# Seven products instead of eight in the second pass of a down projection

## The chip, the cores and the metric

The kernel runs on one core of a Trainium2 chip. The metric is the device time of one execution in microseconds (us). TensorE (PE; its weight loads are PEld) multiplies, VectorE (DVE), ScalarE (ACT) and GpSimd (POOL) work on elements, and SyncE (SP) issues nearly all DMAs from one queue. Every engine takes its instructions in the order of the program.

## The reference

```python
x = A_x                                   # (8192, 448), f32
xn = layernorm(x)
s = irfft2(shrink(relu(rfft2(xn) @ w1 + b1) @ w2 + b2))    # complex, 4 blocks of 112 channels
g = silu((gelu(xn @ w_gate) * (xn @ w_up)) @ w_down)       # 448 -> 1792 -> 448
return x + s * g
```

All arithmetic is as exact as f32: the kernel writes each f32 operand as the sum of two f16 numbers, "high" and "low", and a product as three f16 matmuls (high*high, high*low, low*high) that add up in PSUM.

## The kernel before

Two streams of work share TensorE.

The **feed-forward part** (`ffn`, `chunk`) goes over the tokens in 16 chunks of 512, twice. The first pass takes hidden features 0 to 1023 (8 blocks of 128), the second features 1024 to 1791 (6 blocks, three `unit`s of two blocks). A `unit` makes the up and gate projections of two blocks by a Winograd form of Strassen's scheme: seven products (`product`, a1 to a7) where the plain way has eight; the sums of operands are made beforehand. Its closing steps `c12` and `c21` apply GELU and the gating on ACT and DVE, and write the hidden tile `h` as high and low halves: a cast on ACT (`S.copy`), then a subtraction on DVE or POOL (`B.tensor_sub`). `down` then multiplies `h` with the down weights `dw0` and `dw1` (high, low). In the second pass a chunk has 4 token tiles x 6 blocks x 3 = 72 matmuls with 448 columns each, in `bd` banks. The first pass stores its sums to DRAM (`prt`); the second loads them (`pt_loads`, tile `pt`, two buffers), `ended` adds `bd` to them on DVE, takes tanh on ACT, multiplies on DVE and stores the result to DRAM (`gsp`). Each chunk's transposed tokens come by two transposing DMAs, `xta` and `xtb` (one buffer each).

The **spectral part** runs beside it in three phases. Phase 1 (first pass) normalizes and does the first Fourier stage. Phase 2 (`phase2`, most of the second pass) does the second stage and the spectral MLP in banks `bf`. Phase 3 (`phase3`) loads for each of 32 pairs of columns the spectrum `u2`, a table `mt`, the tokens `x2` and the gate `g2` (from `gsp`), multiplies, adds and stores to `out`. Each phase opens its own pools of tiles where those of the phase before stood.

The order on every engine is set by a planner (`Pace`) while the kernel is built: it keeps an estimated clock for each engine and for DMA (`cost`, line 128 and on), and emits an instruction when its estimate says that the inputs are there; `B` (`Either`) picks DVE or POOL, whichever it expects to end first. Phase 2 is spread evenly up to the planned time `END2`, phase 3 up to `END3`. All instructions are recorded through one helper, line 179, so groups are told apart by tile names.

Of the kernel before, what the change touches and what calls it, by code (L numbers as in the profile page):

```python
# [31 lines left out]
K1, K2 = 256, 192  # L32

# [196 lines left out]

def _split(a):
    hi = a.astype(np.float16)
    lo = (a - hi.astype(np.float64)).astype(np.float16)
    return hi, lo
# [91 lines left out]
def afno_geglu_kernel(ctx, tc, x, gu, wd, mlp, b1, b2, c_m, c_mt, c_small, out):  # L326
# [13 lines left out]
    dsp = nc.dram_tensor("dsp", (128, 2, PF[1][1], D), F16, kind="Internal").ap()  # L340
# [87 lines left out]
    YS = ring(p1, [128, 2, 2, D], F16, "ysb", 2)  # L428
# [5 lines left out]
    XTA = ring(fp, [128, XA // 128, 256], F16, "xta", 1)  # L434
# [7 lines left out]
    PT = ring(fp, [128, D], F32, "pt", 2)  # L442
# [84 lines left out]
    def stage1(c, q, xs):  # L527
# [6 lines left out]
        for a in range(2):  # L534
# [7 lines left out]
            S.activation(ysb[:, a, 0, :], py, AF.Copy, scale=2.0 ** -16)  # L542
            yield
            V.scalar_tensor_tensor(ysb[:, a, 1, :], py, 2.0 ** -16, ysb[:, a, 0, :],
                                   op0=ALU.mult, op1=ALU.subtract)
# [3 lines left out]
        for ri in range(2):  # L549
            Q.dma_start(t1[:, ri, n2:n2 + 2, :], ysb[64 * ri:64 * ri + 64].rearrange("p a s d -> p a (s d)"))  # L550
# [57 lines left out]
    def gu_block(b, to):  # L608
# [23 lines left out]
        S.activation(fc[:, 5, b:b + 1], half[:, 1:2], AF.Copy, scale=2.0 ** -25)  # L632
# [73 lines left out]
    def down_weights(p):  # L706
        fp0, nf = PF[p]
        if p == 0:

            parts, rings, kept = [(0, 4), (4, 2), (6, 2)], {0: WO, 4: XTB, 6: CB}, {}  # L710
        else:
            parts = [(fp0 + k, min(3, nf - k)) for k in range(0, nf, 3)]
# [25 lines left out]
        def split(f, n):  # L738
            t, v = yield from load(f, n)
            if p == 1:  # L740
                do = yield from WO.get()
                dv = do.rearrange("p s v c -> p (s v c)")[:, 0:2 * n * D].rearrange("p (s t c) -> p s t c", s=2, t=n)
            for i in range(n):
                d = [w[:, f + i] for w in dw] if p == 0 else [dv[:, s, i] for s in range(2)]
# [4 lines left out]
                if p == 0:  # L749
                    done("dw", f + i)  # L750
                yield
            (WS if p == 1 else rings[f]).put(t)
            if p == 1:
                Q.dma_start(dsp[:, :, f - fp0:f - fp0 + n, :], dv)
                WO.put(do)
# [18 lines left out]
        V.tensor_scalar(eguv[:, bs], eguv[:, bs], inv, 2.0 ** 14, op0=ALU.mult, op1=ALU.mult)  # L774
        V.tensor_scalar(cB[p], ED, 2.0 ** -11, None, op0=ALU.mult)
# [11 lines left out]
    def far_down():  # L787
        n = PF[1][1]
        for s in range(2):
            Q.dma_start(dw[s][:, 0:n], dsp[:, s])  # L790

    def prep_mlp():

        nonlocal f2, f20, ca, ca0, w1t, w2t, b1s, b2s
# [84 lines left out]
        rm.close()  # L879

# [40 lines left out]
    def glu(p, f0, gl, up, half, h, back):  # L921
        for cs, b in scaled(p, f0):
            V.scalar_tensor_tensor(gl[:, cs], up[:, cs], fc[:, 5, b:b + 1], gl[:, cs],
                                   op0=ALU.mult, op1=ALU.mult)
        back()
        yield
        v = gl.rearrange("p (e c) -> p e c", e=2)
# [5 lines left out]
    def unit(p, i, f0, h, xa, xb):  # L933
# [28 lines left out]
        def a2():  # L962
            m["Z"] = yield from BY.get()
            product(2, m["Z"], xb, f0, True, True)
# [10 lines left out]
        def a3():  # L975
            yield m["ep5"]
            product(3, m["Y"], xb, f0, False, True)
            pace.spawn(c12(), pace.last)

        def c12():  # L980
# [5 lines left out]
            yield m["c11"]  # L986
            yield from glu(p, f0, m["p1"], v, 0, h, lambda: V1.put(v))
# [19 lines left out]
        def a4():  # L1007
            yield m["ev2"]
            product(4, m["X"], xb, f0, False, True)
            pace.spawn(c21(), pace.last)  # L1010

        def c21():
            gl = yield from GL.get()
# [4 lines left out]
            yield from glu(p, f0, gl, m["v2"], 1, h, lambda: V2.put(m["v2"]))  # L1018
            GL.put(gl)
            done("h", p, i, f0, 1)  # L1020

        return [a1, a5, a6, a2, a3, a7], a4
# [40 lines left out]

    def pt_loads(i):
        for a in range(CH):
            t = yield from PT.get()
            Q.dma_start(t, prt[i][:, a * D:(a + 1) * D])
            yield
            EV["ptb", i, a] = t
            done("pt", i, a)  # L1070
# [21 lines left out]
    def ended(p, i, a, b, R):  # L1092
        ps = part(b, 128, D)
        if p == 0:
            th = yield from TH.get()
            S.activation(th, ps, AF.Copy, scale=cB[0])
            R.put(b)
# [640 lines left out]
```

## Time and profile before

| | us |
|---|---|
| median of three runs | 1840.76 (1838.62 to 1842.14) |
| profiled execution, its own time | 1841.37 |
| its span, first to last instruction | 1839.2 |
| TensorE busy | 1792.5 |
| VectorE busy | 1308.5 |
| ScalarE busy | 1061.2 |
| GpSimd busy | 351.6 |

The span is cut by the kernel's own stages: the first pass up to about 750 us; the second pass with phase 2 beside it up to 1500 us; the second pass with phase 3 beside it up to 1800 us; and an end in which the last chunk stands alone. A busy time of TensorE says how long it had a matmul under way; how long one matmul holds the engine is read from the distance between the starts of two groups that follow each other.

### The profile page before, as it was taken

What the parts mean: (1) busy time and instruction counts of PE and PEld (TensorE: products, weight loads), DVE (VectorE), ACT (ScalarE), POOL (GpSimd) and SP (SyncE); (2) the same over time, 40 slices, a digit from 0 to 9 for tenths busy, and PEclk for the clock granted to TensorE, in tenths of its full rate; (3) what the DMA queues carried; (4) which work ended last, traced back from release to release, by engine and by line L of the source; (5) the groups of instructions that cost most, each with busy time, mean ns of one, the idle gap of its engine ahead of it and who ended that gap; (6) DMA issues with size and microseconds to landing.
All of it is one profiled execution on the core that took longest, in us unless ns stands there. A gap on an engine that the chain in (4) does not pass through costs nothing. (4 is left out here: it accounts for less than half of the span.)

```text
span 1839.2 us, 36834 instructions
## 1 busy us (share of the span) xinstructions
PE 1792.5 (97%) x14785; PEld 1345.0 (73%) x14785; DVE 1308.5 (71%) x2271; ACT 1061.2 (58%) x2003; POOL 351.6 (19%) x425
## 2 busy tenths in 40 slices
PE   6999999999999999999999999999999999999998
PEld 3446667766777777787877887788877777777676
DVE  7867888778776665565767777787777766666656
ACT  4745656655555555576777766667766643333343
POOL 3434345325233123000100011010010100000000
PEclk9999999999999999999999999999999999999999
DMA  7463764766445533313235334343254349999872
GB/s 260 144 167 121 214 203 160 230 198 170 132 122 164 152 92 97 78 45 97 64 114 167 113 105 127 97 116 86 74 137 110 88 142 330 301 299 290 294 222 90
DMA packets 319196, 285.58 MB, mean 155 GB/s; under 512 B 230096, under 2 KB 286544, under 8 KB 319024
## 3 DMA queue, kind: packets, MB, share of 16 engines
q1 hardware_dynamic: 318880, 283.19, 52.3%
q8 instruction: 116, 1.90, 0.4%
q14 instruction: 56, 0.46, 0.1%
q10 hardware_dynamic: 144, 0.03, 0.0%
HBM read 128.44 MB, written 105.58 MB: 127 GB/s over the span
## 5 line engine op out<-in xcount | busy, mean ns | idle before, releaser
L179 PEld LDWEIGHTS <-wt 128*128 128x128 f16 x8582 | 836.0, 98 | 185.3 <-issue 19.8
L179 PE MATMUL bd<-dw,h 128*128 128x448 f16 x2592 | 528.6, 352 | 3.5 <-ACT th L179 2.5
L179 PE MATMUL bx<-xta,wt 128*128 128x256 f16 (+1 forms) x3843 | 475.7, 275 | 10.2 <-ACT u L179 4.3
L179 PEld LDWEIGHTS <-h 128*128 128x128 f16 x2592 | 249.9, 98 | 214.3 <-issue 4.1
L179 PE MATMUL by<-xtb,wt 128*128 128x256 f16 x2080 | 250.3, 273 | 0.0
L179 PE MATMUL by<-xta,wt 128*128 128x256 f16 (+1 forms) x1347 | 177.5, 281 | 7.1 <-DVE wt L179 3.1
L179 ACT COPY v<-bx 128x512 f32<-128x512 f32 x208 | 121.3, 583 | 90.9 <-PE bx L179 90.0
L179 DVE SCALAR_TENSOR_TENSOR gl<-v,fc,gl 128x512 f32<-128x512 f32 (+1 forms) x118 | 85.4, 733 | 88.0 <-ACT gl L179 87.3
L179 DVE TENSOR_TENSOR u<-by,u 128x512 f32<-128x512 f32 x104 | 71.6, 688 | 90.9 <-PE by L179 90.8
L179 PE MATMUL bx<-xtb,wt 128*128 128x256 f16 x1040 | 130.6, 273 | 0.3 <-ACT v L179 0.3
L179 POOL TENSOR_TENSOR zs<-t,zs 112x256 f16<-112x256 f32 (+1 forms) x40 | 33.9, 847 | 453.4 <-ACT zs L179 450.8
L179 ACT ACTIVATE gl<-bx,fc 128x512 f32<-128x512 f32 (+1 forms) x118 | 73.6, 637 | 76.4 <-PE bx L179 76.2
L179 ACT ACTIVATE u<-u,fc 128x512 f32<-128x512 f32 (+1 forms) x118 | 77.4, 667 | 60.2 <-DVE u L179 59.7
L179 ACT COPY u<-bx 128x512 f32<-128x512 f32 x104 | 60.7, 584 | 56.1 <-PE bx L179 55.9
L179 DVE SCALAR_TENSOR_TENSOR u<-v,fc,u 128x512 f32<-128x512 f32 (+1 forms) x118 | 87.4, 750 | 6.3 <-ACT u L179 0.8
L179 ACT COPY u<-by 128x512 f32<-128x512 f32 x104 | 60.9, 585 | 51.0 <-PE by L179 44.0
L179 ACT CAST h<-u 128x512 f16<-128x512 f32 x112 | 69.4, 620 | 26.6 <-DVE u L179 25.9
L179 PE MATMUL bf<-w2t,wn 112*128 112x112 f16 x1512 | 84.8, 213 | 0.0
L179 PEld LDWEIGHTS <-wn 112*128 112x128 f16 x1512 | 80.4, 98 | 5.5
L179 ACT ACTIVATE th<-pt 128x448 f32<-128x448 f32 x64 | 36.8, 576 | 77.0 <-DVE pt L179 76.7
L179 DVE SCALAR_TENSOR_TENSOR pt<-bd,fb,pt 128x448 f32<-128x448 f32 x64 | 43.6, 681 | 52.6 <-DMA pt<-prt 33.4
L179 ACT CAST h<-gl 128x512 f16<-128x512 f32 x104 | 64.4, 619 | 27.7 <-DVE gl L179 27.5
(188 smaller groups left out, 2607.0 us busy)
## 6 DMA issues: line engine op xcount, KB each, us to landing
wst<-in_gu SPq DMA_DIRECT2D x22, 704.0 KB, 5.6
xts<-sx SPq DMA_DIRECT2D x32, 480.0 KB, 2.9
x<-in_x SPq DMA_DIRECT2D x17, 896.0 KB, 6.3
t<-ysb SPq DMA_DIRECT2D x64, 224.0 KB, 3.4
prt<-th SPq DMA_DIRECT2D x64, 224.0 KB, 2.7
pt<-prt SPq DMA_DIRECT2D x64, 224.0 KB, 3.6
u<-t SPq DMA_DIRECT2D x32, 448.0 KB, 5.0
y<-t SPq DMA_DIRECT2D x15, 896.0 KB, 5.1
```

Of the source, the lines that this page charges most:

```text
L179: return self.pace.issue(self.name, kind, out, ins, lambda: fn(out, *args, **kw))
```

## The change

- The second pass's down projection takes Strassen's seven products. The hidden tile of two blocks and the two halves of 256 tokens are the left 2x2 matrix; the down weights of two blocks and the two halves of 224 output channels (`DH`) the right one. `factors2` makes the four sums of weights once and stores all seven to DRAM; `far_down` and `far_rest` load them into `dw0`, `dw1` and unused columns of `wt0` to `wt4`. A product of three pairs of blocks is 3 x 2 token tiles x 3 = 18 matmuls with 224 columns: 126 in a chunk.
- The four sums of hidden tiles are made in each unit by `sums`, in f32, in spare columns of `wt7`, and split into high and low halves in `wt6` and `h`. A product's bank is not summed in PSUM alone: `add2` adds a bank to the quarter of `pt` that it belongs to, seven times in a chunk where `ended` did it four times, and some banks go on accumulating after that.
- `down2` issues the first part of a chunk's products after its last unit; the rest (`tail`) stands inside the next chunk's first unit.
- `pt` and `gsp` go by quarters (two token tiles x 224 channels): `pt` has four buffers of half the size. `xta` has a second buffer from the end of phase 1 on, and its next load is issued at a chunk's start rather than at its end.
- Phase 3 has no `o2` buffers any more: its result is written over `g2`, and the store goes out of `g2`.
- Phase 2's planned end goes from 1440 to 1480, phase 3's from 1790 to 1780, and before pools are opened the planner waits 4 or 6 us after the last work. Phase 2's input `y` is loaded in halves of the channels.

```diff
+    def factors2(j, v, sc):
+        S.activation(v, v, AF.Copy, scale=sc)
...
+        B.tensor_sub(c[:, 0], b12, b11)
+        B.tensor_sub(c[:, 2], b22, b12)
+        yield
+        B.tensor_sub(c[:, 1], b22, c[:, 0])
+        yield
+        B.tensor_sub(c[:, 3], b21, c[:, 1])
...
+        Q.dma_start(dsp[:, :, 7 * DH * j:7 * DH * (j + 1)], dv)
...
+    def far_rest():
+        n = dw[0].shape[1] * 2
+        for k in range(n, 7 * PF[1][1] // 2):
+            for s in range(2):
+                Q.dma_start(right(k, s), dsp[:, s, DH * k:DH * k + DH])
...
+        PT = ring(mq, [128, 2, DH], F32, "pt", 4)
+        XTA.put(mq.tile([128, XA // 128, 256], F16, name="xta"))
...
+        def sums(gl):
+            yield ev("h", p, i, f0, 0)
+            g0, x = m["g0"], gl[:, 512:768]
+            a11, a12, a21, a22 = g0[:, 0:256], g0[:, 256:], gl[:, 0:256], gl[:, 256:512]
+            B.tensor_add(x, a21, a22)
+            S.copy(h[:, f0 + 1, 0, 256:], a22)
+            yield
+            B.tensor_sub(a21, a11, a21)
+            B.tensor_sub(a11, x, a11)
+            yield
+            B.tensor_sub(a12, a12, a11)
...
+            S.copy(w[0], v)
+            yield
+            S.copy(hs[0][:, 0], g0)
+            B.tensor_sub(w[1], v, w[0])
+            B.tensor_sub(h[:, f0 + 1, 1, 256:], a22, h[:, f0 + 1, 0, 256:])
...
+            B.tensor_sub(hs[1][:, 0], g0, hs[0][:, 0])
...
+    def prod2(k, i, h, bank_, j0, j1, first=False, last=False):
+        (e, c), r = PROD2[k]
+        for j in range(j0, j1):
...
+            for t in range(2):
+                for n, (s, v) in enumerate(((0, 0), (0, 1), (1, 0))):
+                    T.matmul(bank_[:, DH * t:DH * t + DH], w[s][:, 128 * t:128 * t + 128], right(7 * j + r, v),
+                             start=first and j == 0 and t == 0 and n == 0,
+                             stop=last and j == 2 and t == 1 and n == 2, skip_group_check=True)
+            yield pe()
+    def add2(i, q, bank_):
+        yield ev("pt", i, q)
+        t = EV["ptb", i, q]
+        V.scalar_tensor_tensor(t, part(bank_, 128, 2, DH), cB[1], t, op0=ALU.mult, op1=ALU.add)
+        yield
+    def down2(i, h, last):
+        yield from last()
+        x = yield from BD.get()
+        yield from prod2(1, i, h, x, 0, 2, first=True)
+        z = yield from BY.get()
+        yield from prod2(2, i, h, z, 0, 2, first=True)
+        y = yield from BD.get()
+        yield from prod2(5, i, h, y, 0, 2, first=True)
+        yield from prod2(1, i, h, x, 2, 3)
+        e = pace.spawn(add2(i, QS[0], x), pace.last)
+        yield from prod2(2, i, h, z, 2, 3, last=True)
+        yield e
+        pace.spawn(ended2(i, QS[0], z, BY), pace.last)
+        yield from prod2(6, i, h, x, 0, 2)
+        def tail():
+            yield from prod2(5, i, h, y, 2, 3)
+            e5 = pace.spawn(add2(i, QS[1], y), pace.last)
+            yield from prod2(6, i, h, x, 2, 3)
+            e = pace.spawn(add2(i, QS[2], x), pace.last)
+            yield e5
+            yield from prod2(3, i, h, y, 0, 2)
+            yield e
+            yield from prod2(7, i, h, x, 0, 3)
+            pace.spawn(ended2(i, QS[1], x, None), pace.last)
+            yield from prod2(3, i, h, y, 2, 3, last=True)
+            pace.spawn(ended2(i, QS[2], y, BD), pace.last)
+            yield ev("u3", i)
+            yield from prod2(4, i, h, x, 0, 3, last=True)
+            pace.spawn(ended2(i, QS[3], x, BD), pace.last)
...
         yield ev("xt", "a", p, i)
+        if p == 1 and nxt:
+            pace.spawn(xt_load(nxt[1], "a", nxt[0]))
...
             for n, s in enumerate(six):
+                if (u, n) == (0, 2) and "tail" in state:
+                    yield from state.pop("tail")()
...
-    END1, END2, END3 = T1 + NG * DT + 12.0, 1440.0, 1790.0
+    END1, END2, END3 = T1 + NG * DT + 12.0, 1480.0, 1780.0
...
-            V.scalar_tensor_tensor(o2[:, a, :], p, cF, t[3][:, a, :], op0=ALU.mult, op1=ALU.mult)
+            V.scalar_tensor_tensor(o2[:, a, :], p, cF, o2[:, a, :], op0=ALU.mult, op1=ALU.mult)
...
-            P3["g2"].put(t[3])
             Q.dma_start(ov[:, 2 * c:2 * c + 2, :], o2)
-            P3["o2"].put(o2)
+            P3["g2"].put(o2)
```

TensorE at the end of a chunk of the second pass, before. `bd` is the bank of the down projection, `h` the hidden tile (weights of the array), `dw0` and `dw1` the down weights; `vt` and `sm` belong to phase 2, `bx` and `xta` to the next chunk's first unit.

```order
L179 MATMUL bd_16424<-dw0_84,h_15680 128x448
L179 LDWEIGHTS h_15680
L179 MATMUL bd_16424<-dw1_85,h_15680 128x448
...
L179 LDWEIGHTS sm_4502
L179 MATMUL bf_16469<-vt_16413,sm_4502 128x448
...
L179 LDWEIGHTS wt0_76
L179 MATMUL bx_16481<-xta_16195,wt0_76 128x256
```

The chunk's down projection ends before the next chunk's first product. TensorE at such a place now, where product 2 ends in bank `by_13710` and product 6 goes on in bank `bd_13682`, which holds product 1; `wt6` holds sums of hidden tiles:

```order
L180 MATMUL by_13710<-dw0_84,h_12297 128x224
L180 LDWEIGHTS h_12297
L180 MATMUL by_13710<-dw1_85,h_12297 128x224
L180 LDWEIGHTS h_12297
L180 MATMUL by_13710<-dw0_84,h_12297 128x224
L180 LDWEIGHTS wt6_82
L180 MATMUL bd_13682<-dw0_84,wt6_82 128x224
```

Each matmul has half the columns and still its own weight load, and a bank goes on from `h` to the sums in `wt6`, after `add2` has read it.

SP in phase 3, before: one pair of columns' loads (`u2`, `mt`, `x2`, `g2`) and its store, with the second pass's `gsp`, `pt` and `xta` between.

```order
L179 DMA g2_20188<-gsp 128x896
L179 DMA out_0<-o2_20190 128x896
L179 DMA gsp<-th_20275 128x448
L179 DMA pt_20309<-prt 128x448
L179 DMA u2_20311<-t2 128x2x896
L179 DMA mt_20313<-c_mt 128x768
L179 DMA x2_20315<-in_x 128x896
L179 DMA g2_20317<-gsp 128x896
L179 DMA out_0<-o2_20319 128x896
L179 DMA_TRANSPOSE xta_20425<-xts 128x16x256
```

The same queue now; `g2` is both loaded and stored.

```order
L180 DMA pt_21120<-prt 128x2x224
L180 DMA_TRANSPOSE xtb_21148<-xts 128x9x256
L180 DMA g2_21163<-gsp 128x896
L180 DMA out_0<-g2_20952 128x896
L180 DMA u2_21191<-t2 128x2x896
L180 DMA mt_21193<-c_mt 128x768
L180 DMA x2_21195<-in_x 128x896
L180 DMA_TRANSPOSE xta_94<-xts 128x16x256
L180 DMA out_0<-g2_21032 128x896
```

A load of `g2` now stands behind an earlier store out of the buffer that it takes, and `xta` and `xtb` of a chunk are apart.

## Rows read from the trace of the kernel before

**Rows 1.** The page, part 1: busy time, share and instructions of each engine.

```profile
PE 1792.5 (97%) x14785; PEld 1345.0 (73%) x14785; DVE 1308.5 (71%) x2271; ACT 1061.2 (58%) x2003; POOL 351.6 (19%) x425
```

**Rows 2.** Busy time by stretch: length, PE, PEld, DVE, ACT, POOL, clock, DMA, GB/s.

```profile
700.00:800.00 100.00, 96.80 (x823) 73.42 (x822) 54.81 (x107) 52.86 (x108) 13.41 (x11) 1.00 0.35 92
800.00:1400.00 600.00, 600.00 (x5831) 489.17 (x5830) 441.55 (x762) 422.82 (x840) 60.34 (x57) 1.00 0.39 105
1400.00:1500.00 100.00, 98.70 (x957) 80.50 (x955) 73.58 (x132) 65.10 (x135) 10.06 (x11) 1.00 0.30 80
```

**Rows 3.** Timeline of PE, second pass, phase 2 beside it: start, length, group.

```profile
1104.72 1.34 PE L179 MATMUL bf<-w2t,wn 112*128 112x112 f16 x24
1105.90 1.26 PE L179 MATMUL by<-xtb,wt 128*128 128x256 f16 x10
...
1116.78 3.00 PE L179 MATMUL bd<-dw,h 128*128 128x448 f16 x15
1119.62 0.49 PE L179 MATMUL bf<-zs,w1t 112*112 112x256 f16 x3
...
1131.69 1.48 PE L179 MATMUL bx<-xta,wt 128*128 128x256 f16 x12
1133.00 1.47 PE L179 MATMUL by<-xta,wt 128*128 128x256 f16 x12
```

**Rows 4.** Weight loads by form, whole span: count, busy us, mean ns.

```profile
L179 PEld LDWEIGHTS <-h 128*128 128x128 f16 x2592 | 249.9, 98 | 214.3 <-issue 4.1 <-POOL h L179 1.4 <-DVE h L179 0.2
```

**Rows 5.** What PE waited for after 500 us: total, times, longest.

```profile
PE bx L179 <- ACT u L179: 2.7, 3, 2.0
PE bx L179 <- DMA xta<-xts: 1.8, 1, 1.8
```

**Rows 6.** DVE groups by form, 1000 to 1400 us: count, busy us, mean ns.

```profile
L179 DVE SCALAR_TENSOR_TENSOR pt<-bd,fb,pt 128x448 f32<-128x448 f32 x25 | 17.0, 681 | 10.3 <-PE bd L179 8.6 <-PE bf L179 0.9 <-DMA pt<-prt 0.8
...
L179 DVE TENSOR_TENSOR k<-bf,k 112x256 f32<-112x256 f32 x36 | 15.1, 420 | 5.2 <-ACT k L179 4.4
...
L179 DVE TENSOR_TENSOR h<-gl,h 128x512 f16<-128x512 f32 x21 | 14.3, 682 | 0.3 <-ACT h L179 0.3
```

**Rows 7.** ACT groups by form, the same stretch.

```profile
L179 ACT CAST h<-gl 128x512 f16<-128x512 f32 x21 | 13.0, 618 | 1.9 <-DVE gl L179 1.9
```

**Rows 8.** POOL groups by form, whole span.

```profile
L179 POOL TENSOR_TENSOR sf<-sf,x 128x256 f32<-128x256 f32 x23 | 29.3, 1273 | 25.1 <-ACT sf L179 24.0 <-ACT u L179 0.9
...
L179 POOL TENSOR_TENSOR sf<-x 128x256 f32<-128x256 f32 x16 | 14.5, 906 | 0.3 <-DVE x L179 0.3
```

**Rows 9.** Timeline of all engines around the longest stop of PE in phase 3.

```profile
1701.31 0.68 DVE L179 SCALAR_TENSOR_TENSOR pt<-bd,fb,pt 128x448 f32<-128x448 f32 x1 [4.83 <-DMA pt<-prt]
...
1702.03 0.58 ACT L179 ACTIVATE th<-pt 128x448 f32<-128x448 f32 x1 [10.12 <-DVE pt L179]
...
1703.13 1.65 PE L179 MATMUL bx<-xta,wt 128*128 128x256 f16 x7 [2.01 <-ACT u L179]
```

**Rows 10.** Busy time by stretch, phase 3, columns as in rows 2.

```profile
1500.00:1580.00 80.00, 77.62 (x574) 55.94 (x573) 50.05 (x76) 27.43 (x46) 6.84 (x5) 1.00 1.03 336
1580.00:1780.00 200.00, 196.45 (x1462) 143.58 (x1460) 131.31 (x206) 73.44 (x124) 4.67 (x3) 0.99 0.91 279
...
1500.00:1800.00 300.00, 294.07 (x2176) 213.33 (x2175) 191.03 (x296) 108.39 (x183) 11.52 (x8) 0.99 0.93 290
```

**Rows 11.** Timeline at the start of phase 3: its first load and first matmul.

```profile
1500.28 0.34 SPq L179 DMA_DIRECT2D x4l<-in_x  x1
...
1510.13 0.73 PE L179 MATMUL bf<-u,mt 128*128 128x448 f16 x3
```

**Rows 12.** Timeline at the end: the last matmuls and the last sum.

```profile
1820.79 11.51 PE L179 MATMUL bd<-dw,h 128*128 128x448 f16 x60
...
1833.15 0.68 DVE L179 SCALAR_TENSOR_TENSOR pt<-bd,fb,pt 128x448 f32<-128x448 f32 x1 [0.41 <-DMA pt<-prt]
...
1835.24 0.62 DVE L179 TENSOR_TENSOR th<-th,x4l 128x448 f32<-128x448 f32 x1
```

More of the change, by code (lines that the diff above doesn't have):

```diff
@@ L228, in put, with __init__, get @@
             self.free.append(t)
+class Slots:
+    def __init__(self, pace, views):
+        self.pace, self.free, self.waiting = pace, [(0.0, v) for v in views], []
+    def get(self):
+        if self.free:
+            t, view = self.free.pop(0)
+        else:
+            event = Event()
+            self.waiting.append(event)
+            yield event
+            t, view = event.at
+        if t > self.pace.now:
+            yield t
+        return view
+    def put(self, view):
+        t = self.pace.ready(view, True, None)
+        if self.waiting:
+            event = self.waiting.pop(0)
+            event.at = t, view
+            self.pace.set(event)
+        else:
+            self.free.append((t, view))
 def _split(a):
@@ new lines, in ended2 @@
+    def ended2(i, qq, b, R):
+        yield from add2(i, qq, b)
+        if R:
+            R.put(b)
+        else:
+            done("u3", i)
+        q = EV["ptb", i, qq]
+        tf = yield from TH.get()
+        th = tf.rearrange("p (a d) -> p a d", a=2)
+        S.activation(th, q, AF.Tanh)
+        yield
+        if i < NG - 1:
+            V.scalar_tensor_tensor(th, th, 1.0, q, op0=ALU.add, op1=ALU.mult)
+            PT.put(q)
+            yield
+            Q.dma_start(blk(chunk_of(gsp, i), *qq), th)
+            TH.put(tf)
+            EV["gn", i] = EV.get(("gn", i), 0) + 1
+            if EV["gn", i] == 4:
+                done("gsp", i)
+            return
+        for a in range(qq[0], CH, 2):
+            yield ev("s4", a)
+        s4, x4 = (blk(t, *qq) for t in state["last"])
+        V.tensor_tensor(s4, q, s4, op=ALU.mult)
+        V.scalar_tensor_tensor(th, th, 1.0, s4, op0=ALU.add, op1=ALU.mult)
+        V.tensor_add(th, th, x4)
+        PT.put(q)
+        yield
+        Q.dma_start(blk(ov[:, CH * i:CH * i + CH, :], *qq), th)
+        TH.put(tf)
@@ L1204, in chunk, with rest @@
         XTA.put(xa)
-        if nxt:
+        if nxt and p == 0:
             pace.spawn(xt_load(nxt[1], "a", nxt[0]))
         cut = nf - 2
+        def rest():
+            yield from prev()
+            XTB.put(EV["xtb", p, i])
+            if (p, i) == (0, NG - 1):
+                pace.spawn(far_pair(nf // 2 - 1))
+            if nxt:
+                pace.spawn(xt_load(nxt[1], "b", nxt[0]))
+            yield pe()
+        if p == 1:
+            yield from down2(i, h, rest)
+            if not nxt:
+                yield from state.pop("tail")()
+            return
         yield from down(p, i, 0, 0, cut, hv)
         yield pe()
-        yield from prev()
-        XTB.put(xb)
-        if (p, i) == (0, NG - 1):
-            pace.spawn(far_pair(nf // 2 - 1))
-        if nxt:
-            pace.spawn(xt_load(nxt[1], "b", nxt[0]))
-        yield pe()
+        yield from rest()
         yield from down(p, i, 1, 0, cut, hv)
@@ L1508, in phase2 @@
             yield ev("t2", g)
+        yield pace.last + 4.0
     P3 = {}
@@ L1533, in tiles3 @@
         u2, mt = t[0:2]
-        o2 = (yield from P3["o2"].get()) if c < 2 * NG - 2 else None
+        o2 = t[3] if c < 2 * NG - 2 else None
         for a in range(2):
@@ L1688, in weights @@
         yield pace.spawn(down_weights(1))
+        far_rest()
+        yield pace.last + 6.0
         yield pace.spawn(prep_mlp())
```

216 lines of the change are left out of this document (125 added, 91 removed).

## The prediction

> **What bounds the kernel now.** I read the page's busy times first, then busy times by stage, then PE's timeline, its waits, and DMA by stage. The page has TensorE busy for 1792.5 of 1839.2 us [rows 1]. That is a mean over stages, so the stages come next: beside phase 2 PE is busy for 600.00 of 600.00 us, with VectorE at 441.55 (74%) and ScalarE at 422.82 (70%) [rows 2]. Nothing else can bound there; what is to be gained is matmul time, and what is to be lost is any wait that reaches PE. A busy figure doesn't say how long one matmul holds the engine, since the latency of one overlaps the next; the starts do. Fifteen matmuls of 448 columns take 1119.62 - 1116.78 = 2.84 us, 189.3 ns each; twelve of 256 take 1.31 us, 109.2 ns; twenty-four of 112 take 1.18 us, 49.2 ns [rows 3]. All three lie on one line: 0.417 ns a column (2.4 GHz) and 2.5 ns more per matmul.
>
> Phase 3 is another stage: PE is busy for 294.07 of 300 us, and the DMA engines are at 0.93 of their time, at 290 GB/s [rows 10]. There PE's idle time is what the transfers leave. One stop shows how [rows 9]: a `pt` load is late, VectorE waits 4.83 us for it, ScalarE's tanh stands 10.12 us behind that, the copy that frees a bank stands behind the tanh, and PE stops for 2.01 us. The granted clock, 1.00 elsewhere, has a mean of 0.99 over the 200 us that hold this stop, about 2 us lost. After 500 us the stops on ACT's `u` and on `xta` come to 4.5 us [rows 5].
>
> **The change part by part.** The sum is made against the profiled execution's own 1841.4 us (1839.2 and 2.2 around it), 0.6 over the median.
>
> *Matmuls of the down projection.* Removed: 72 x 16 = 1152 at 189.3 ns, 218.1 us. Added: 126 x 16 = 2016 of 224 columns. No row has this size; on the line of rows 3 it takes 49.2 + 112 x 0.417 = 95.9 ns, so 193.3 us. All of it is on the path, since PE has no idle time to hide in: -24.8 us. The bounds of the pitch are the neighbours, 49.2 and 109.2 ns; at 109.2 ns the added ones would cost 220.2 us and the gain would be gone. The other limit is the weight load that each matmul has for itself: one shows 98 ns [rows 4], longer than 95.9. But twenty-four matmuls of 49.2 ns also each have a weight load, so loads overlap; I take 95.9.
>
> *Sums of hidden tiles.* A unit wrote its second half with a cast and a subtraction. Now it makes four sums of 256, four casts for three (three of 512 for two, one of 256) and four subtractions for two. At 682 ns for a subtraction of 512 and 420 ns for one of 256 [rows 6] that is 0.68 + 5 x 0.42 = 2.78 us a unit, 8.3 a chunk, if all were on VectorE; three more `pt` sums at 681 ns make 10.4 us in a chunk of about 55. ScalarE gets 618 ns [rows 7] and a cast of 256 of about 0.4, 3.1 us a chunk. The order gives about half of the small sums to POOL (its rows go from 413 to 610), where one takes 906 or 1273 ns [rows 8]. So VectorE goes from 74% to something like 80%, at worst 91%, and ScalarE to 75%. The chain from a unit's last product to the weights of product 5 is gelu and gating (some 0.7 us each), two or three sums, a cast and a subtraction: 5 to 7.3 us, as the sums go to VectorE or POOL. Counted in the order, some 11 us of matmuls stand between the two (that is what holding the tail back to the next chunk buys), so it is hidden; if a chain were late, all of PE behind it would be. Bounds: 0, and 2 us a chunk (four sums each 0.5 us slower on POOL than the planner's line for it, 0.2 us and 2.3 ns an element), 32 us. I take 3, near the bottom, because 600 us without one stop say that the planner's lead is worth several us.
>
> *`add2` between products of one bank.* PE must wait for VectorE's 681 ns to read a bank before the next product goes on in it. Beside phase 2 and 3 the order puts other matmuls there; in the last chunk nothing is left to put. Covers there are 6 or 12 matmuls, 0.58 or 1.15 us, against 0.17 us of drain, 0.68 and two signals: about 0.4 us short at three places. The last sum runs as before: the last matmul ends at 1832.3, then `pt`, tanh, two products and a sum end at 1835.86 [rows 12]; three quarters close to each other may queue on VectorE. Together +2 us (0 to 4).
>
> *Weights, `y` halves, pools.* `factors2` and ten small loads run in the first pass, beside PE's own work; PE there waits for neither. The 3.2 us that PE idles between 700 and 800 us, where phase 2 opens [rows 2], may go or not: 0, bounds -4.5 and +3.
>
> *Phase 3.* It now begins later and ends earlier. Between the first matmul on `mt` and the end PE had 737,856 columns in 2349 matmuls, 313 us; now 608,640 in 2328, 259 us; between the first and the last one on `mt` it is 248. Phase 3's own 61.7 thousand KB of loads and stores are all still there. What goes is the second pass's share: SP's queue has 7 pairs of `xta` and `xtb`, 30 `pt` and 28 `gsp` loads and stores behind phase 3's first load before, and 5 pairs, 24 and 24 of them now. In all 87.9 MB fall to 82.4 MB. The time for it is 10 us of lead (first load at 1500.28, first matmul at 1510.13 [rows 11]), 248, less about 5 for the last load: 253 us. At the mean rate of 290 GB/s it would need 284; at the 336 GB/s of the first 80 us, where loads were asked for as fast as they came [rows 10], 245. So the stage is full to the brim. I take the dense rate, since that is the row where DMA and not PE set the pace, and 9 us of idle where there were 5.9 and some 2 of low clock. The causes of those are cut: `pt` gets loads a chunk ahead and `xta` a second buffer. So +1.1 us (-7.9 to +34, below).
>
> Sum: 1841.4 - 24.8 + 3 + 2 + 0 + 1.1 = 1822.7; against the median, 1822.
>
> On the pitch the Trainium skill has a rule against this change: "TensorE: Matmul & The Clock Gate", section "Back-to-back issue gap", says that in a stream of pairs of weight load and matmul one costs about 81 ns at 128 columns and 131 ns at 512, so that columns are cheap and matmuls dear. On that line 224 columns cost 93.5 ns and 448 cost 123, and a chunk would lose 126 x 93.5 - 72 x 123 = 2.9 us, 47 us in all. This trace differs: 189.3 ns at 448 and 49.2 at 112 are such pairs.
>
> **The rivals.**
>
> *A. DMA sets phase 3's time (slower).* If the queue gives only the 279 GB/s of 1580 to 1780 us [rows 10], 82.4 MB take 295 us against 253: 42 us of idle in place of 7.9, 1841.4 - 24.8 + 3 + 34.1 = 1854. It decides from about 286 GB/s down. For it: DMA is at 0.91 even there; a load of `g2` has to wait for the store out of its buffer, on the queue that also issues `xta`. Against: in that stretch PE set the pace, and 336 GB/s were had at a share of 1.03.
>
> *B. The sums are late (no change).* Each chunk loses 1.2 us because small sums on POOL take 1273 ns where the planner allows some 790: 19 us, 1841.4 - 24.8 + 19 + 2 + 1.1 = 1839. For it: POOL was nearly idle here (60 of 600 us) and is now asked for three times that. Against: the 11 us of cover.
>
> *C. Weight loads bound the small matmuls (faster, by less).* At 98 ns instead of 95.9 the gain falls by 2016 x 2.1 ns = 4.2 us: 1826. If loads did not overlap at all it would be no gain at all. Against: the 49.2 ns. By the Trainium skill's rule above, which I give one chance in a hundred of C's five, the time would be some 1890.
>
> *D. All waits vanish.* Phase 3's 7.9 us go, and nothing new comes but the last chunk's 2: 1841.4 - 24.8 - 7.9 + 2 = 1811.
>
> **How the numbers follow.** Forecast (1814 to 1832) 0.62; D 0.10; C 0.05, of which a small part is no gain; B 0.12; A 0.11. Within 0.2% (about what a measurement of this kernel can tell from no change) is 1837.1 to 1844.4. Faster: 0.62 + 0.10 + 0.04 and a quarter of B, 0.80. Slower: 0.08 of A. The rest, 0.12, is the same. Range 1810 to 1842: it leaves out the worst of A and a little of D.
>
> **What would show it.** In the trace after: matmuls `bd<-dw,h` and `bd<-dw,wt` of 224 columns with 95 to 97 ns between starts (98 or more: C); PE without idle beside phase 2, and VectorE near 80% there (stops of PE on VectorE, ACT or POOL with `h` or `wt6` as their tile: B); in phase 3 DMA at 1.0 and over 320 GB/s, with no stop behind `pt` or `xta` (stops of PE on `u`, `mt` or of VectorE on `g2`, and a rate of 280 to 290: A); about 2 us of small stops on `bd` in the last chunk. The prediction is wrong at its root if the distance between starts isn't on the line of rows 3, and wrong in its sum if phase 3 idles for more than 20 us.

## The result: 0.36% slower, where 1% faster was forecast

The kernel after takes 1848.6 us (median of five runs, 1845.2 to 1850.9), the one before 1842.1 in the same set: a ratio of 1.0036, 95% interval 1.0024 to 1.0047. The forecast was 1822. Some 25 us were to be won by matmuls; 31 us have to be found on the other side.

**The matmul term first.** The page's first part and the timeline of PE in the kernel after (start, length, group; in brackets idle time before and what ended it):

```profile
PE 1780.5 (96%) x15649; PEld 1426.4 (77%) x15649; DVE 1418.0 (77%) x2412; ACT 1098.5 (59%) x2105; POOL 565.7 (31%) x635
```

```profile
1217.84 0.49 PE L180 MATMUL bf<-z,w1t 112*112 112x256 f16 x3 [1.24 <-DVE k L180]
1218.16 1.31 PE L180 MATMUL bd<-dw,wt 128*128 128x224 f16 x12
1219.32 0.74 PE L180 MATMUL bd<-dw,h 128*128 128x224 f16 x6
1219.89 0.83 PE L180 MATMUL bf<-sm,y 128*112 128x128 f16 x12
```

Eighteen matmuls of 224 columns take 1219.89 - 1218.16 = 1.73 us, 96.1 ns each; the line of [rows 3] gave 95.9. Over the whole span, 1765 such distances between two matmuls that follow each other at the full granted clock have a mean of 95.9 ns. The busy time of [rows 1] fell by 12 us only: it also holds the latency of the last matmul before each stop, and the stretches at a lower granted clock, so the starts are what to read. What a reader should see above all is the bracket in the first row: PE stops beside phase 2, where it had none in 600 us [rows 2]. POOL went from 351.6 to 565.7 us and VectorE from 1308.5 to 1418.0.

**The stops.** Busy time by stretch of the kernel after (columns as in [rows 2]), and what PE waited for after 800 us (total, times, longest):

```profile
700.00:800.00 100.00, 99.90 (x837) 76.43 (x836) 57.33 (x113) 52.65 (x106) 18.28 (x21) 1.00 0.34 87
800.00:1400.00 600.00, 595.40 (x6178) 524.30 (x6176) 474.23 (x808) 427.63 (x861) 136.09 (x138) 1.00 0.41 106
...
800.00:1500.00 700.00, 693.96 (x7257) 614.83 (x7255) 559.14 (x949) 501.91 (x1016) 179.10 (x177) 1.00 0.41 105
...
1500.00:1600.00 100.00, 94.36 (x886) 82.43 (x885) 79.25 (x126) 49.34 (x98) 32.69 (x32) 0.98 0.77 218
...
1700.00:1800.00 100.00, 94.43 (x820) 79.87 (x819) 81.17 (x118) 40.96 (x73) 35.20 (x32) 0.98 0.93 302
...
1580.00:1780.00 200.00, 188.46 (x1648) 160.49 (x1647) 165.39 (x242) 81.85 (x145) 72.57 (x65) 0.99 0.97 303
1500.00:1800.00 300.00, 285.31 (x2564) 245.75 (x2563) 241.82 (x367) 129.96 (x241) 99.14 (x91) 0.99 0.88 271
```

```profile
PE bd L180 <- DVE pt L180: 9.0, 21, 2.0
PE bd L180 <- DVE h L180: 4.5, 4, 1.9
PE bf L180 <- DVE k L180: 3.1, 4, 1.2
PE bx L180 <- ACT v L180: 2.8, 3, 1.3
PE bd L180 <- ACT h L180: 2.5, 3, 1.2
PE bd L180 <- POOL h L180: 0.8, 1, 0.8
PE bx L180 <- ACT u L180: 0.5, 1, 0.5
```

VectorE is at 79% beside phase 2 (474.23 of 600), as forecast. In phase 3 it is at 81% (241.82 of 300; 64% in [rows 10]), and POOL at 33% (4%). PE is busy for 285.31 of 300 us there, 8.8 us less than in [rows 10], and not one stop is on a DMA: a share of 0.97 at 303 GB/s is enough. The listed stops add up to 23.2 us after 800 us. The largest item, 21 stops of `bd` behind `pt`, is VectorE reading a bank (`add2`) before PE may go on in it; the next is the hidden values `h`. Two of the 21, the second with VectorE's read:

```profile
1640.69 1.31 PE L180 MATMUL bd<-dw,wt 128*128 128x224 f16 x12 [1.78 <-DVE pt L180]
...
1835.62 1.31 PE L180 MATMUL bd<-wt,h 128*128 128x224 f16 x12
1836.39 1.28 DVE L180 SCALAR_TENSOR_TENSOR pt<-bd,fb,pt 128x448 f32<-128x448 f32 x2 [1.98 <-PE bd L180]
...
1837.13 1.31 PE L180 MATMUL bd<-dw,h 128*128 128x224 f16 x12 [0.20 <-DVE pt L180]
```

A product's last six matmuls open the run at 1835.62, and six of the other bank follow. VectorE begins to read behind the first six, so only the other six (0.58 us) cover the read. PE then idles for 0.20 us; from start to start the run takes 1.51 us in place of 1.15, so 0.36 us are lost. Sixteen of the 21 stops are of this kind. Five are longer (0.58 to 2.00 us): there VectorE was still at other work when the bank was ready.

**The first pass**, on which the prediction put no cost, holds a stop of 5.17 us that was not there before. Timeline of SP's queue, ScalarE and PE there:

```profile
440.97 0.56 SPq L180 DMA_DIRECT2D dsp<-wo  x1
...
444.86 4.62 SPq L180 DMA_DIRECT2D wt<-dsp  x10
...
453.69 1.40 SPq L180 DMA_DIRECT2D prt<-th  x2
...
457.38 1.16 ACT L180 ACTIVATE th<-bd,fb 128x448 f32<-128x448 f32 x2 [14.51 <-DMA prt<-th]
...
458.90 0.61 ACT L180 COPY u<-by 128x512 f32<-128x512 f32 x1
459.07 2.72 PE L180 MATMUL bx<-xta,wt 128*128 128x256 f16 x12 [5.17 <-ACT u L180]
```

The ten loads of `far_rest` stand on SP's queue in front of the stores of the partial results. They first wait for the store `dsp<-wo` that they read, and then take 4.62 us to issue, so the queue is held for 8 us, from 441.5 to 449.5. ScalarE has two `th` buffers, waits 14.51 us for a store to free one (6.68 us at this place in the kernel before), and its copies out of the banks, which PE needs, stand behind that. Twelve matmuls of 256 columns then show 2.72 us, and the granted clock from 459 to 464 us is 0.50: PE comes out of the stop at the lower level, 1.2 GHz.

**What VectorE does beside POOL.** Groups of VectorE by form, from 800 us to the end (count; busy us, mean ns; idle time before), and a timeline of one stop in phase 3:

```profile
L180 DVE TENSOR_TENSOR v<-by,v 128x512 f32<-128x512 f32 x60 | 41.0, 683 | 5.6 <-PE by L180 4.9
...
L180 DVE TENSOR_TENSOR v<-v,u 128x512 f32<-128x512 f32 x48 | 39.0, 813 | 0.8 <-ACT v L180 0.8
```

```profile
1586.73 0.73 DVE L180 SCALAR_TENSOR_TENSOR wt<-v,fc,u 128x512 f32<-128x512 f32 x1
1586.89 1.57 POOL L180 TENSOR_TENSOR g<-g,x 128x448 f32<-128x448 f32 x1 [1.55 <-DVE g L180]
...
1587.39 1.61 DVE L180 SCALAR_TENSOR_TENSOR wt<-v,fc,wt 128x512 f32<-128x512 f32 x1
...
1588.93 0.67 DVE L180 SCALAR_TENSOR_TENSOR g<-bf,ms,g 128x448 f32<-128x448 f32 x1
...
1589.52 0.83 DVE L180 TENSOR_TENSOR h<-wt,h 128x512 f16<-128x512 f32 x1
...
1590.41 0.85 PE L180 MATMUL bd<-dw,h 128*128 128x224 f16 x4 [1.88 <-DVE h L180]
```

The same form of 512 columns takes 683 ns where one operand is a bank and 813 where both are in SBUF. In the timeline the gating that begins before POOL's sum `g<-g,x` takes 0.73 us, though the two overlap for most of it; the next one begins while that sum runs and takes 1.61. VectorE comes to phase 3's `g` and then to the subtraction `h` late, and PE's stop of 1.88 us is behind that `h`.

All of VectorE's sums and gatings of 256 and 512 columns from 800 us on, sorted by what POOL did, show the same (mean ns and count, from the trace of the kernel after):

| columns, operands | POOL idle | POOL begins during it | POOL at work when it begins |
|---|---|---|---|
| 512, both in SBUF | 706 (213) | 702 (37) | 1142 (71) |
| 512, one in a bank | 685 (99) | 684 (26) | 684 (53) |
| 256, both in SBUF | 426 (89) | 482 (15) | 868 (45) |
| 256, one in a bank | 415 (79) | 409 (9) | 413 (28) |

Against the median of its own form with POOL idle, what began beside POOL took 71 us longer in all between 800 and 1800 us, and 17 us in the kernel before: an estimate from the two traces, and about half of the 113 us by which the durations of VectorE's operations grew together there. The Trainium skill, "SBUF — State Buffer", section "Who interferes with whom", has this as a rule: a VectorE instruction with two SBUF inputs contends with a GpSimd instruction that reads SBUF, and one with at most one SBUF input doesn't, outside some modes of copies, casts and `tensor_scalar`. The trace agrees, with 1142 against 706 ns for two operands in SBUF and 684 against 685 for one.

### The profile page after: what moved, and what is told of

The parts are those of the page before. It is cut to its first block, busy times and chain, and to the rows that moved or that the text cites. A ratio compares the mean times of both kernels' runs of the same rounds, so it can differ in the third digit from the quotient of the medians.

```text
span 1847.1 us, 39099 instructions
## 1 busy us (share of the span) xinstructions
PE 1780.5 (96%) x15649; PEld 1426.4 (77%) x15649; DVE 1418.0 (77%) x2412; ACT 1098.5 (59%) x2105; POOL 565.7 (31%) x635
## 5 line engine op out<-in xcount | busy, mean ns | idle before, releaser
L180 PEld LDWEIGHTS <-wt 128*128 128x128 f16 x9350 | 910.0, 98 | 198.1 <-issue 35.1
L180 PEld LDWEIGHTS <-h 128*128 128x128 f16 x2688 | 258.6, 98 | 142.4 <-DVE h L180 7.2
L180 PE MATMUL bd<-dw,h 128*128 128x448 f16 (+1 forms) x1920 | 345.1, 329 | 11.1 <-DVE h L180 5.3
L180 POOL TENSOR_TENSOR wt<-wt 128x256 f32<-128x256 f32 x100 | 85.2, 852 | 236.9 <-DVE wt L180 163.6
L180 POOL TENSOR_TENSOR zs<-t,zs 112x256 f16<-112x256 f32 (+2 forms) x38 | 29.8, 785 | 294.0 <-ACT zs L180 293.9
L180 PE MATMUL bd<-dw,wt 128*128 128x224 f16 (+1 forms) x816 | 96.6, 268 | 8.1 <-DVE pt L180 8.0
L180 ACT CAST h<-wt 128x512 f16<-128x512 f32 (+1 forms) x128 | 68.7, 538 | 51.8 <-DVE wt L180 43.9
L180 DVE SCALAR_TENSOR_TENSOR pt<-bd,fb,pt 128x448 f32<-128x448 f32 x96 | 63.8, 678 | 33.3 <-PE bd L180 32.8
L180 ACT ACTIVATE th<-bd,fb 128x448 f32<-128x448 f32 x62 | 39.0, 632 | 80.3 <-PE bd L180 46.7
L180 POOL TENSOR_TENSOR v<-v,u 128x512 f32<-128x512 f32 x33 | 47.4, 1435 | 123.8 <-ACT v L180 123.1
```

The costliest lines, as they stand in the source:

```text
L180: return self.pace.issue(self.name, kind, out, ins, lambda: fn(out, *args, **kw))
```

## The experiments

All times are medians; the ratio is to the kernel before, run on the same chip beside them (1841.4 to 1842.1 us). E1 to E4 change one thing of the kernel after. Differences between two rows are taken from the ratios, since each group of runs had its own times of the kernel before; such a difference is known to some 3 us.

| | us | ratio, 95% |
|---|---|---|
| kernel after | 1848.6 | 1.0036 (1.0024 to 1.0047) |
| E1 loads later | 1844.5 | 1.0014 (1.0005 to 1.0023) |
| E2 sums on VectorE | 1866.4 | 1.0140 (1.0125 to 1.0156) |
| E3 due times as before | 1859.9 | 1.0096 (1.0081 to 1.0110) |
| E4 no sums | 1837.2 | 0.9979 (0.9970 to 0.9988) |
| E6 tail in three pieces | 1837.3 | 0.9983 (0.9972 to 0.9994) |
| E7 = E1 + E6 | 1833.6 | 0.9961 (0.9950 to 0.9973) |
| E8 = E7, other durations | 1840.8 | 1.0001 (0.9989 to 1.0012) |
| E9 = E8, shared | 1842.3 | 1.0011 (1.0000 to 1.0021) |
| E10 = E7, no sums | 1821.9 | 0.9886 (0.9873 to 0.9899) |
| E11 before + POOL work | 1846.9 | 1.0026 (1.0015 to 1.0037) |
| E13 = E7, durations from 700 us | 1835.2 | 0.9957 (0.9943 to 0.9971) |
| E14 = E7, sum from the bank | 1834.2 | 0.9955 (0.9942 to 0.9968) |

**E1, the loads at the end of the first pass.**

```
             far_down()
+            far_rest()
...
         yield pace.spawn(down_weights(1))
-        far_rest()
```

> The ten loads of the second pass's last down weights are issued at the end of the first pass, with the other down weights, and not in its middle. Theory (they hold SP's queue for 8 us, the partial results are stored late, ScalarE stands 14.5 us behind that store, and PE 5.2 us behind ScalarE): no stop of PE of over 1 us between 440 and 480 us, no low clock there, and 6 to 9 us less, about 1841 us. Rival (ScalarE is late there for another reason): the stop stays and the time is within 2 us of 1848.6. Rival (the loads only move their cost): the stop is gone, a new one on the down weights stands at the start of the second pass, and the time is within 3 us of 1848.6.

What PE waited for between 430 and 480 us in E1:

```profile
...
PE by L180 <- ACT u L180: 1.3, 1, 1.3
PE bf L180 <- DVE mxr L180: 1.2, 1, 1.2
...
```

The stop of 5.2 us and the low clock are gone, no new stop stands at the start of the second pass, and 0.22% (4 us) are won. That is less than the 6 to 9 expected: stops of 1.3 and 1.2 us stand there that the kernel after didn't have, and the stops after 800 us come to 26.0 us in this run's trace, against 23.2.

**E2, the sums on VectorE alone.** In `sums`, `B` becomes `V` in all seven places, the first of them:

```
-            B.tensor_add(x, a21, a22)
+            V.tensor_add(x, a21, a22)
```

> The small sums and subtractions of each hidden unit's second half all go to VectorE, none to POOL. Theory S (while POOL works, VectorE's operations between two tiles in SBUF take longer, so what was given to POOL slows both, and the gated values and the sums on the banks come late in phase 3): VectorE's mean for the gating returns to some 680 ns, its busy share rises a little, the stops of PE after 1500 us fall by half or more, and the time falls by 8 to 14 us, to about 1837. Rival V (VectorE is simply full, whoever shares): VectorE goes to 90% beside phase 2, PE stops on it there too, and the time rises by 5 to 25 us, 1854 to 1874.

```profile
800.00:1500.00 700.00, 686.30 (x7122) 603.84 (x7121) 575.40 (x1007) 496.14 (x1003) 113.66 (x94) 1.00 0.40 103
1500.00:1800.00 300.00, 282.37 (x2556) 243.87 (x2554) 254.18 (x419) 131.81 (x244) 62.09 (x45) 0.99 0.88 270
```

The forecast of theory S fell: the time rose by 19 us against the kernel after, in the range of rival V. VectorE rose to 82% beside phase 2 (not 90%) and to 85% in phase 3, and PE lost 8 and 3 us more. So VectorE's load counts, and these seven operations cost more on VectorE alone than shared with POOL. The price of sharing this run doesn't show, for it hardly took the sharing away: POOL still had 176 us of other work between 800 and 1800 us (278 in the kernel after), the first half's gating took 886 ns on the mean in place of 927 and not 680, and by the estimate above VectorE's operations still lost 65 us beside POOL, against 71.

**E3, due times as before.**

```
-    END1, END2, END3 = T1 + NG * DT + 12.0, 1480.0, 1780.0
+    END1, END2, END3 = T1 + NG * DT + 12.0, 1440.0, 1790.0
```

> The due times that the planner gives the end of phase 2 and of phase 3 are put back to those of the kernel before (1440 and 1790 in place of 1480 and 1780). Theory (the late operations come from the sums, not from the density of phase 3): the stops beside phase 2 grow a little or stay, those in phase 3 fall by a third at most, and the time is within 4 us of 1848.6. Rival (phase 3 is pressed into too short a time, so that its own operations on VectorE and POOL collide with the second pass): stops of PE after 1500 us fall by two thirds, and the time falls by 10 to 15 us, to about 1836.

```profile
800.00:1500.00 700.00, 684.32 (x7085) 602.70 (x7084) 551.91 (x931) 484.33 (x987) 178.22 (x163) 1.00 0.40 103
```

Neither: 11 us slower. PE is busy for 684.32 us of these 700 in place of 693.96. Phase 2 pressed into 40 us less costs more than a looser phase 3 gives. The rival (phase 3 too dense) is out, for PE's stops after 1500 us come to 16.3 us against 17.5, and not to a third. The kernel before had the same due times and no such loss beside phase 2.

**E4, without the four sums.**

```
-            B.tensor_add(x, a21, a22)
...
-            B.tensor_sub(a21, a11, a21)
-            B.tensor_sub(a11, x, a11)
...
-            B.tensor_sub(a12, a12, a11)
-            v = gl.rearrange("p (k c) -> p k c", k=3)[:, 0:3:2]
+            v = gl[:, 0:512].rearrange("p (k c) -> p k c", k=2)
```

> Left out are the four sums of 256 columns that make the combined hidden tiles (the casts and subtractions to two halves stay, and so do all matmuls). Theory (the sums' load on VectorE and POOL makes the gated values and the sums on the banks late): PE's stops between 800 and 1500 us fall from 9 to under 4 us, those after 1500 us from 28 to 10 to 15 us, and the time falls by 15 to 20 us, to about 1831. Rival (phase 3's own transfers and operations make the stops): the time falls by under 5 us, 1844 or more.

```profile
PE bd L180 <- DVE pt L180: 12.7, 28, 2.1
...
PE bd L180 <- POOL h L180: 0.2, 1, 0.2
```

The time falls by 0.57%, 10.5 us; between the two theories. The stops on `h` go but for 0.2 us, so those came with the sums. The stops behind `pt` stay and grow, from 21 to 28: they belong to the order of the products and not to the sums. That led to E6. Leaving the sums out lightens VectorE and POOL and also shortens the chain to `h`; E4 and E10 price the two together.

**E6, the tail in three pieces.**

```
-                if (u, n) == (0, 2) and "tail" in state:
-                    yield from state.pop("tail")()
+                if u == 0 and n in (2, 3, 4) and state.get("tail"):
+                    yield from state["tail"].pop(0)()
...
+        def tail1():
+            yield e
+            yield from prod2(6, i, h, x, 0, 2)
             yield from prod2(5, i, h, y, 2, 3)
...
             yield from prod2(6, i, h, x, 2, 3)
...
+        def tail2():
+            yield es[5]
             yield from prod2(3, i, h, y, 0, 2)
...
             yield from prod2(7, i, h, x, 0, 3)
...
+        def tail3():
             yield from prod2(3, i, h, y, 2, 3, last=True)
...
             yield from prod2(4, i, h, x, 0, 3, last=True)
...
+        state["tail"] = [tail1, tail2, tail3]
```

The first part of product 6, which `down2` issued itself, goes into the first piece as well.

> The tail of a chunk's down projection is cut in three, and each piece stands between two products of the next chunk's first unit (12 matmuls of 256 columns, 1.3 us, between two pieces). So other matmuls always stand between a product and the next one in the same bank. Theory W (PE waits for VectorE to read the bank between two products; that is 9.0 us of stops of bd behind pt after 800 us in the changed kernel, where the prediction had 2): these stops fall under 2 us, and the time falls by 5 to 8 us, to about 1842. Rival (VectorE is late as such, and the bank is only where it shows): the stops turn up on other tiles, and the time is within 3 us of 1848.6.

What PE waited for after 800 us, and phase 3 by its busy times, in E6:

```profile
PE bf L180 <- DVE k L180: 5.1, 6, 1.6
PE bx L180 <- ACT v L180: 4.9, 5, 1.6
...
PE bd L180 <- DVE pt L180: 1.9, 2, 1.7
...
```

```profile
1500.00:1800.00 300.00, 292.79 (x2706) 256.82 (x2704) 255.38 (x387) 141.15 (x263) 103.37 (x94) 1.00 0.87 273
```

Theory W holds, and gives a little more than it promised: 0.53%, 9.8 us. The stops behind `pt` go from 9.0 us to 1.9, and those that are left stand after 1800 us. Some turn up elsewhere (`bx` behind `v`: 2.8 to 4.9; `bf` behind `k`: 3.1 to 5.1), as the rival had it. All stops together go from 23.2 to 16.3 us. In phase 3 the granted clock is 1.00 again; in the kernel after it was 0.98 in two stretches of 100 us there, about 2 us each. VectorE is at 85% in phase 3 (255.38 of 300), more than in the slower kernel after, so its share alone doesn't say what PE will wait for.

**E7, both.** The edits of E1 and E6.

> The loads at the end of the first pass and the tail in three pieces, together. If the two costs stand apart, the gains of the two single kernels add up: 4 us and 5 to 8 us, about 1838. If each gain is taken back by VectorE being late further on, it is within 3 us of the better of the two.

0.75%, 13.8 us less than the kernel after: 4.1 and 9.8 add up. It beats both kernels, by 0.39% the one before.

**E8 and E9, other durations for the planner**; E9 also books POOL's overlap on VectorE.

```
-            return max(0.049, n * 0.00042 + 0.001) * (4 if ins[0].dtype == F32 and op == "matmul" else 1)
+            return (n * 0.000417 + 0.0025) * (4 if ins[0].dtype == F32 and op == "matmul" else 1)
...
-            return 1.1 if n < 8 and op == "tensor_tensor_pow" else 0.2 + 0.0023 * n
+            return 1.1 if n < 8 and op == "tensor_tensor_pow" else 0.32 + 0.0021 * n
...
-            return 0.12 + 0.00112 * n + min(busy, 0.5 + 0.0005 * n)
+            base = 0.14 + 0.00115 * n
+            return base + min(0.6 * busy, 1.4 * base)
...
-        return 0.14 + 0.00107 * n
+        return 0.16 + 0.0011 * n
```

> As e7, and the planner's table of durations is set to the means of the changed kernel's trace: a matmul 0.417 ns a column and 2.5 ns, POOL 0.32 us and 2.1 ns an element, VectorE's sums of two SBUF tiles up to 2.4 times as long while POOL works (0.685 us alone against up to 1.64 us for 512 columns). Theory P (the order is made with durations that are too short, so that what PE waits for stands too close ahead of it): stops of PE after 800 us fall to half of e7's, and the time falls by a further 5 to 12 us. Rival (VectorE and POOL have no time left whatever the order): within 4 us of e7.

```
+            if e == "POOL" and self.shared and self.free.get("DVE", 0.0) > start:
+                self.free["DVE"] += 0.6 * (min(self.free["DVE"], end) - start)
...
```

> As e8, and work booked on POOL also delays what VectorE already has, by 0.6 of the overlap. This gives POOL some 150 more of the small operations. Theory P: 2 to 6 us better than e8, since the slowing is seen from both sides. Rival (each operation on POOL slows VectorE by as much as it takes off it): 3 us or more slower than e8.

Theory P fell: 7 and 9 us slower than E7. A good part of it is the first pass, whose order the table sets too (PE is busy for 383.4 us from 100 to 500 us in E8, 387.3 in E7), so E13 set it from 700 us on. E9 gives POOL 149 more operations than E8 (780 against 631), and shows no difference from it beyond the intervals.

**E13, durations from 700 us.** For POOL, and likewise for the others:

```
-            return 1.1 if n < 8 and op == "tensor_tensor_pow" else 0.2 + 0.0023 * n
+            return 1.1 if n < 8 and op == "tensor_tensor_pow" else (0.2 + 0.0023 * n if start < 700.0 else 0.32 + 0.0021 * n)
```

> As e7, with the planner's table of durations set to the trace's means only from 700 us on (in e8 the new table also made the first pass's order worse: 12 us of stops between 300 and 400 us). Theory P (an order made with true durations has fewer late operands): 3 to 6 us less than e7, about 1829. Rival (VectorE's load itself, not the order): within 2 us of e7.

The same as E7 within the intervals. Durations nearer to the trace, in this table, do not make an order with fewer late operands; that another table could is not excluded. (Between 300 and 400 us the trace of E8 has 6.2 us of stops and a granted clock of 0.95, where the expectation speaks of 12 us of stops.)

**E10, E7 without the four sums.**

> As e7, and the four sums of 256 columns that make the combined hidden tiles are left out (casts, subtractions and matmuls stay). If the three costs (loads in the first pass, waits for a bank, the sums) are all that took the matmuls' gain, the time is that of the kernel before less 17 to 21 us: 1821 to 1825. If the stops are rooted elsewhere (phase 3's own work, the greater number of other small operations), it falls by under 4 us from e7, to 1830 or more.

What PE waited for after 800 us, and its phase 3:

```profile
PE bf L180 <- DVE k L180: 3.8, 5, 1.4
PE bx L180 <- ACT v L180: 1.8, 2, 1.4
PE bd L180 <- DVE pt L180: 1.3, 1, 1.3
PE bd L180 <- DVE h L180: 1.0, 2, 0.6
```

```profile
1500.00:1800.00 300.00, 297.28 (x2743) 261.23 (x2741) 234.37 (x358) 139.27 (x262) 65.89 (x56) 1.00 0.88 283
```

1821.9 us, 1.14% (21.0 us) under the kernel before and 0.75% (13.8 us) under E7. The stops are down to 7.9 us (7.2 in the kernel before), and PE is busy for 297.28 of 300 us in phase 3. Three costs account for nearly all that took the gain.

**E11, the kernel before with work on POOL**, once for each hidden unit of the second pass.

```
...
+                z = wt[7][:, 0, 0:8].rearrange("p v c -> p (v c)").bitcast(F32)
...
+                for _ in range(3):
+                    nc.gpsimd.tensor_add(z[:, 0:256], z[:, 0:256], z[:, 256:512])
```

> The kernel before, with three sums of 256 columns for each hidden unit of the second pass added on POOL, on a scratch tile that nobody reads: 144 in all, about 120 us of POOL's time. VectorE's instructions stay the same. Theory S (POOL's work by itself slows VectorE's sums of two SBUF tiles, and that reaches PE): VectorE's operations of two SBUF tiles that fall beside them take 1.0 us and more in place of 0.685, those that read a bank stay at 0.68, PE gets stops on VectorE after 800 us, and the time rises by 4 to 12 us. Rival (VectorE at 74% has the room): the same slowing, but under 2 us in time; then the sharing costs only together with the added load.

A timeline of VectorE and POOL, and what PE waited for after 800 us:

```profile
1107.67 0.75 DVE L179 SCALAR_TENSOR_TENSOR gl<-v,fc,gl 128x512 f32<-128x512 f32 x1 [1.74 <-ACT gl L179]
...
1118.77 3.13 POOL L1025 TENSOR_TENSOR wt<-wt 128x256 f32<-128x256 f32 x3
...
1120.09 1.21 DVE L179 SCALAR_TENSOR_TENSOR gl<-v,fc,gl 128x512 f32<-128x512 f32 x1
1121.22 0.41 DVE L179 TENSOR_TENSOR k<-bf,k 112x256 f32<-112x256 f32 x1
```

```profile
PE bf L179 <- DVE k L179: 2.4, 6, 0.5
```

Theory S holds in its weaker form: nothing waits for these sums and VectorE's instructions are the same, yet the time rises by 0.26%, 4.8 us, at the low end of what was expected (2.8 to 6.8 us by the interval, so the rival's 2 us are out). The gating takes 0.75 us alone and 1.21 beside them, the sum on a bank 0.41 in the same stretch, and six stops on `k` are new. PE never waits for POOL there, and VectorE's and ScalarE's waits for POOL hardly change (6.3 us in the kernel before, 7.3 here), so POOL's own operations standing behind these sums are hardly the cause. By the estimate above VectorE's operations lost 43 us beside POOL, against 17 in the kernel before. So of the sums' cost a part is probably mere sharing. How the 10.5 to 13.8 us divide between sharing and VectorE's added load wasn't settled: from 800 to 1800 us POOL has 134 us more work in E11 than in the kernel before, and 196 more in the kernel after.

**E14, the second half's sum straight from the bank.**

```
+            if p == 1:
+                V.tensor_tensor(m["v2"], m["X"], m["p5"], op=ALU.add)
+                pace.set(m["ev2"])
...
```

> As e7, and in the second pass the sum of the second half's up projection is made by VectorE straight from the bank (0.685 us, with one operand in SBUF only), in place of a copy by ScalarE and a sum of two SBUF tiles on VectorE or POOL. Theory S (sums of two SBUF tiles are what POOL and VectorE slow each other by): VectorE's busy share stays within 3 points though it takes the sums that POOL had, POOL's falls, and the time falls by 2 to 5 us from e7. Rival (VectorE's load is what counts): VectorE's share rises by over 3 points and the time by 2 to 8 us.

The same as E7 within the intervals: neither theory. VectorE's share did stay within 3 points (79% and 84% beside phases 2 and 3, 80% and 85% in E7), but POOL's hardly fell (273 us against 283) and the time didn't. PE's stops on `bx` now name VectorE (6.2 us) where they named ScalarE (4.0).

## Why the prediction was wrong

The gain was forecast rightly, by its mechanism and its size. What failed are three costs: the prediction put +3 us on the sums, +2 on `add2` and nothing on the weights' loads, 5 us together, and the runs price them at 13.8, 9.8 and 4.1 us, some 28 together.

- *Matmuls, -24.8 us*: right. 96.1 ns on the chip; E10 has 21.0 of the 24.8 us left with the three costs away. Rival C is out. The Trainium skill's rule in "TensorE: Matmul & The Clock Gate", section "Back-to-back issue gap", which by the prediction's estimate gives 93.5 ns at 224 columns and 123 at 448 and would have made this a loss, does not hold for these pairs: 96.1 and 189.3 ns.
- *`add2`, +2 (0 to 4)*: **failed, in the places counted**. The working said: "Beside phase 2 and 3 the order puts other matmuls there". So it counted only three places in the last chunk. There are 21 stops: 6 beside phase 2 (2.1 us), 12 in phase 3 (4.0) and 3 in the last chunk (2.9). The price of a place, some 0.4 us, was right: sixteen lose about 0.36 us from start to start, behind six matmuls. The other five are longer, since VectorE came late. E6 prices the step at 9.8 us with the clock that comes back.
- *Sums of hidden tiles, +3 (0 to 32)*: the outcome was named (rival B), **the value mis-sized**: 10.5 us alone (E4), 13.8 beside the other repairs (E10). "600 us without one stop" was read as lead to spend, but with the new work VectorE went from 74% to 79% beside phase 2 and from 64% to 81% in phase 3, and the 600 us had stops. The mechanism was not B's: POOL's own sums took 852 ns on the mean, near the planner's 790 and not 1273. The prediction did not look at what POOL does to VectorE. The added load was right (79%).
- *Weights, 0 (-4.5 to +3)*: **failed**. "PE there waits for neither" looked at PE's operands and not at what stands behind ten loads on SP's queue. 4.1 us (E1); the idle time where phase 2 opens went, as could be (96.80 in [rows 2], now 99.90).
- *Phase 3, +1.1*: **the wrong resource**. The prediction weighed DMA (rival A); the transfers held at 303 GB/s without one stop of PE. It did not ask what VectorE, 64% there before, would be at with the new sums and with POOL beside it. From the first matmul on `mt` (1553.5 us) to the last matmul of all PE idles for 16.6 of 285.5 us, where the sum had 9; its own sign of failure, over 20 us, was not met, because the loss was spread over the other stages too. E3 shows that phase 3's due times weren't at fault.
- *The last chunk*: as expected in kind. Its stops behind `pt` are 2.00, 0.67 and 0.20 us, and the three last quarters queue on VectorE, so that the end comes 8 us after the last matmul's, in place of 7 (the third stop is shown above):

```profile
1834.47 1.31 PE L180 MATMUL bd<-dw,wt 128*128 128x224 f16 x12 [0.67 <-DVE pt L180]
...
1843.50 0.62 DVE L180 TENSOR_TENSOR th<-th,x4l 128x448 f32<-128x448 f32 x1
```

The account by the experiments: -24.8 + 4.1 + 9.8 + 13.8 = +2.9 us, where +6.6 was measured. The 3.7 us between stay open; they are not much more than the 3 us to which each step is known. Taken from the medians as they stand, E10 is 11.7 us under E7 and not 13.8. How the sums' price divides between load, sharing with POOL and the longer chain to `h` is open as well. Two slips in the prediction's working changed nothing: rival A's sum leaves out the 2 us of `add2`, and a unit makes four casts for two, not for three.

## What to carry to other kernels

When an accumulation in a bank is read between two products, count for every such place the matmuls that stand between, against the latency of the last matmul and the whole read (here 0.58 us against 0.94, which is 0.58 and the 0.36 lost), in every stage and not only at the end. Before work goes to POOL, ask which of VectorE's operations have both operands in SBUF: those that begin while POOL works take longer, and that time belongs in the sum. And a load that nobody waits for still stands in front of what is issued behind it on its queue: follow the queue, not only the operand.

## What was not expected of the hardware

Who begins first decided here. In the kernel after, VectorE operations of 512 columns with both operands in SBUF took 706 ns on the mean with POOL idle, 702 where POOL began during them, and 1142 where POOL was already at work; with one operand in a bank it was 684 or 685 ns in all three cases. In E11 POOL's sums of 256 columns on a tile that nobody else used cost the whole kernel 0.26%. And a stop is dearer than its length: after the 5.17 us stop PE ran at a granted clock of 0.50 for 5 us more, and each of the short stops loses 0.16 us beyond the idle time that is shown for it.
